# A linear-attention and SoLU kernel: the conversion of the weights, the decay tables, the attention diagonals, the load queues and the order of the last iterations are changed

## The chip, the cores and the metric

The kernel runs on one core of one Trainium2 chip. The core has five engines with a queue of instructions each: TensorE (PE; its weight loads are shown apart as PEld), VectorE (DVE), ScalarE (ACT), GpSimd (POOL) and SyncE (SP), which here only issues transfers. Transfers run on 16 DMA engines. The time is the device time of the program in microseconds (us); the median of three runs before the change is 511.51 us (511.32 to 512.56).

## The reference, cut to what matters

```python
batch, n_heads, seq, head_dim = (4, 8, 768, 48)       # r, k, v
n_tokens, d_model, d_ff = (3072, 384, 1024)           # w_in, w_out, g_ln: float64 weights, float32 gain
...
for t in range(S):
    cur = np.einsum('bhd,bhe->bhde', u[None] * kt, vt)
    y[:, :, t] = np.einsum('bhd,bhde->bhe', rt, state + cur)
    state = w[None, :, :, None] * state + np.einsum('bhd,bhe->bhde', kt, vt)
...
h = x @ w_in
e = np.exp(h - h_max)
solu = h * e / (np.sum(e, axis=-1, keepdims=True) + 1e-09)
ln = (solu - mu) / np.sqrt(var + 1e-06) * g_ln
return (ln @ w_out).astype(np.float32)
```

First a linear attention with a decay w per head and channel runs over 768 steps of four sequences. Its output, 3072 tokens of 384, goes through a feed-forward block: a matmul to 1024, an activation h·softmax(h), a layer norm with a gain, and a matmul back to 384. The two weight matrices arrive as 64-bit floats and are turned into 32-bit ones on the chip.

## The kernel before

The work is cut into 24 units of 128 tokens: unit i is one sequence (b) and one chunk (c) of the 768 steps, with c in the outer loop, so that four units of one chunk follow each other. `direct_path` holds everything that runs; another path is entered at the end only if a decay lies outside 0.75 to 1.25.

Ahead of the loop, tables are built (lines 537 to 556). `wd` holds the decay, one channel to a partition, loaded by two transfers of single words. Squarings give its powers `pw`; `back` is the decay to the powers 127 down to 0, built by doubling its columns seven times; `fore` is the reciprocal of `back` times the decay; `kdec` is `back` transposed on PE.

Each unit passes these steps:

- `load` (454): k, r and v of the unit on SP's queue, 192 KB each in rows of 192 bytes.
- `weigh` (592): POOL forms `kp`, the weighted keys (596), and `rku` (600, 601); DVE sums it to `own` (603); POOL writes `AT`, a diagonal of `own` for each of eight heads (605).
- `turn` (608): PE transposes r (`tr_ps`) and kp (`tk_ps`); DVE scales the first by `fore` into `rT` (615), ACT copies the second into `kT` (619).
- `scores` (622): 16 small matmuls into two tiles `at`; DVE copies what lies above the diagonal into `AT` (632).
- `finish` (635): the matmuls `y_ps` from the state (643) and from `AT` and v (648), an ACT copy to `x` (652), the matmuls `kv_ps` (656) and the new state.
- `turn_x` (665): transposes of x, and an ACT copy to `xT` (671).
- `ffn_in` (673): 12 matmuls of 512 columns into `h_ps` (678); then maximum, exp, sum and product on DVE and ACT, with two one-column steps on POOL, into `solu`.
- `turn_ln` (700): transposes of `solu` (`t_ps`), and copies to `lnT` on DVE (708) and ACT (710).
- `ffn_out` (712): matmuls of 384 columns into `o_ps` (717), an ACT copy (720) and a store on SP's queue (721).

The loop (730) runs i from -2 to 31 and does these steps for different units: the attention of unit i, `ffn_in` five units behind (LA) and `ffn_out` another three behind (LO). So the feed-forward input of unit 0 comes in iteration 5, the output in iteration 8, and the attention ends in iteration 23. PE's order is the order in which the program is written (`manual_schedule`, 729). On the other engines and queues the framework's scheduler chooses the order by the program's order and by what it takes to be ready; each runs its list strictly in that order.

Between `turn` and `ffn_in`, iterations from -1 on convert two pieces of the weights each (738): six pieces of w_in (128 x 512) and then eight of w_out (128 x 384). A raw piece comes by a transfer on ACT's queue (495) into one of five buffers; `convert` (497) takes the exponent and mantissa out of the two 32-bit words with seven DVE instructions, and POOL adds the low part (521, 523) and, for w_out, multiplies by the gain (524).

## Time and profile before

| | |
|---|---|
| median of three runs | 511.51 us |
| the profiled execution | 512.92 us |
| its span, first to last instruction | 511.1 us |
| busy PE / PEld / DVE / ACT / POOL | 440.5 / 304.0 / 263.8 / 119.5 / 189.0 us |
| the same, share of the span | 86 / 59 / 52 / 23 / 37 % |
| mean granted clock of PE | 0.938 of 2.4 GHz |
| moved by DMA | 25.84 MB, 50 GB/s of HBM over the span |

The span is shorter than the profiled execution by 1.8 us, which lie around it. The page cuts the span in 40 slices and writes a digit for each engine and slice, the busy share in tenths (9 is 90% or more). The granted clock is given in the same way: 9 stands for full speed, 5 for half. "Idle before, releaser" names what ended an engine's idle time. A chain of waits leads from the last instruction back to what released each step.

### The profile page before, as it was taken

What the parts mean: (1) busy time and instruction counts of PE and PEld (TensorE: products, weight loads), DVE (VectorE), ACT (ScalarE), POOL (GpSimd) and SP (SyncE); (2) the same over time, 40 slices, a digit from 0 to 9 for tenths busy, and PEclk for the clock granted to TensorE, in tenths of its full rate; (3) what the DMA queues carried; (4) which work ended last, traced back from release to release, by engine and by line L of the source; (5) the groups of instructions that cost most, each with busy time, mean ns of one, the idle gap of its engine ahead of it and who ended that gap; (6) DMA issues with size and microseconds to landing.
All of it is one profiled execution on the core that took longest, in us unless ns stands there. A gap on an engine that the chain in (4) does not pass through costs nothing.

```text
span 511.1 us, 5767 instructions
## 1 busy us (share of the span) xinstructions
PE 440.5 (86%) x2220; PEld 304.0 (59%) x2220; DVE 263.8 (52%) x441; ACT 119.5 (23%) x217; POOL 189.0 (37%) x193
## 2 busy tenths in 40 slices
PE   0147776795999999999999999999999898888995
PEld 0137766772777757766776667666765564444453
DVE  4999999996763443345244425432443123333310
ACT  0110001012242332322232223222322222222211
POOL 2797668589554235324532442232000000000000
PEclk9995557597999999999999999999999999999999
DMA  9972436122222022212211221000000000000001
GB/s 193 249 135 58 112 91 149 33 48 47 48 47 62 16 47 62 49 29 47 63 37 36 51 48 32 1 17 15 17 2 14 15 17 15 16 11 5 15 32 38
DMA packets 81991, 25.84 MB, mean 51 GB/s; under 512 B 76961, under 2 KB 80162, under 8 KB 81954
## 3 DMA queue, kind: packets, MB, share of 16 engines
q1 hardware_dynamic: 78336, 18.88, 17.8%
q10 hardware_dynamic: 3618, 6.50, 4.2%
q8 instruction: 19, 0.31, 0.3%
q14 instruction: 18, 0.15, 0.1%
HBM read 20.65 MB, written 4.72 MB: 50 GB/s over the span
## 4 chain that ended last, share of the span: by engine, by line
PE 68%; DVE 22%; DMA 4%; POOL 2%; ACT 1%; issue 1%; ACTq 0%; DVEq 0%; POOLq 0%
PE o_ps L717 25%; PE h_ps L678 22%; PE y_ps L648 6%; PE at L629 3%; PE y_ps L643 3%; PE kv_ps L656 3%; PE t_ps L706 2%; DVE low L518 2%; DVE st L682 2%; DVE ex L507 2%; DVE ma L515 2%; DVE ma L517 2%; DVE ex L508 2%; DVE ex L510 2%; DVE AT L632 2%; DMA rpad<-in_r_dram 2%
## 5 line engine op out<-in xcount | busy, mean ns | idle before, releaser
L678 PE MATMUL h_ps<-w_in_sb,xT 128*128 128x512 f32 x288 | 129.9, 601 | 10.3 <-DVE solu L688 5.9
L717 PE MATMUL o_ps<-w_out_sb,lnT 128*128 128x384 f32 x384 | 130.3, 492 | 8.0 <-DVE lnT L708 8.0
L717 PEld LDWEIGHTS o_ps<-w_out_sb,lnT 128*128 128x128 f32 x384 | 71.0, 190 | 56.8 <-DVE lnT L708 10.5
L678 PEld LDWEIGHTS h_ps<-w_in_sb,xT 128*128 128x128 f32 x288 | 53.4, 192 | 70.6 <-issue 64.4
L693 POOL TENSOR_SCALAR st<-st 128x1 f32<-128x1 f32 x24 | 4.6, 192 | 206.6 <-ACT sq L692 206.3
L682 DVE TENSOR_REDUCE st<-h_ps 128x1 f32<-128x1024 f32 x24 | 29.4, 1223 | 75.4 <-PE h_ps L678 75.4
L605 POOL TENSOR_TENSOR AT<-ident,own 128x1024 f32<-128x1024 f32 x24 | 46.5, 1938 | 46.2 <-PE y_ps L648 41.7
L648 PE MATMUL y_ps<-vt,AT 128*128 128x48 f32 x384 | 54.3, 302 | 0.0
L648 PEld LDWEIGHTS y_ps<-vt,AT 128*128 128x128 f32 x384 | 52.9, 221 | 0.8 <-issue 0.7
L629 PE MATMUL at<-rT,kT 48*128 48x128 f32 x384 | 35.2, 318 | 18.2 <-DVE AT L632 18.1
L696 DVE TENSOR_SCALAR solu<-solu,st 128x1024 f32<-128x1024 f32 x24 | 20.8, 869 | 54.6 <-POOL st L695 54.6
L629 PEld LDWEIGHTS at<-rT,kT 48*128 48x128 f32 x384 | 29.6, 215 | 25.5 <-DVE AT L632 15.4
L710 ACT COPY lnT<-t_ps 128x512 f32<-128x512 f32 x24 | 14.1, 586 | 121.6 <-PE t_ps L706 121.0
L692 ACT ACTIVATE sq<-solu,st 128x1024 f32<-128x1024 f32 x24 | 27.5, 1148 | 51.7 <-DVE st L690 51.7
L596 POOL TENSOR_TENSOR kp<-kpad,kdec 128x512 f32<-128x512 f32 x24 | 34.2, 1428 | 12.4 <-PE kv_ps L656 12.4
L632 DVE COPY_PREDICATED AT<-later,at 128x512 f32<-128x512 uint32 x48 | 33.5, 724 | 1.8
L603 DVE TENSOR_REDUCE own<-rku 128x8 f32<-128x384 f32 x24 | 13.1, 545 | 38.6 <-POOL rku L601 38.6
L652 ACT COPY x<-y_ps 128x384 f32<-128x384 f32 x24 | 11.5, 479 | 90.4 <-PE y_ps L648 90.4
L688 DVE SCALAR_TENSOR_TENSOR solu<-h_ps,st,e 128x1024 f32<-128x1024 f32 x24 | 30.8, 1284 | 0.8
L684 ACT ACTIVATE e<-h_ps,st 128x1024 f32<-128x1024 f32 x24 | 26.9, 1119 | 15.4 <-DVE st L682 15.4
L706 PEld LDWEIGHTS t_ps<-ident,solu 128*128 128x128 f32 x192 | 22.5, 141 | 12.0 <-issue 10.2
L600 POOL TENSOR_TENSOR rku<-kpad,u_bc 128x384 f32<-128x384 f32 x24 | 25.6, 1066 | 9.6 <-DMA kpad<-in_k_dram 9.1
(67 smaller groups left out, 489.6 us busy)
## 6 DMA issues: line engine op xcount, KB each, us to landing
kpad<-in_k_dram SPq DMA_DIRECT2D x24, 192.0 KB, 3.5
rpad<-in_r_dram SPq DMA_DIRECT2D x24, 192.0 KB, 3.3
vt<-in_v_dram SPq DMA_DIRECT2D x24, 192.0 KB, 2.9
out_dram<-o SPq DMA_DIRECT2D x24, 192.0 KB, 1.9
raw<-in_moe_w_in_dram ACTq DMA_DIRECT2D x6, 512.0 KB, 6.2
raw<-in_moe_w_out_dram ACTq DMA_DIRECT2D x8, 384.0 KB, 3.8
u_bc<-in_u_dram ACTq DMA_DIRECT2D x1, 192.0 KB, 3.9
wd<-in_w_dram ACTq DMA_DIRECT2D x2, 0.8 KB, 6.0
```

Source lines behind the costliest of these rows:

```text
L596: nc.gpsimd.tensor_mul(kp.rearrange("p h d -> p (h d)"), kt.rearrange("p h d -> p (h d)"), kdec.rearrange("p a d -> p (a d)"))
L605: nc.gpsimd.tensor_mul(AT, ident.unsqueeze(1).to_broadcast([128, H, T]), own.to_broadcast([128, H, T]))
L629: nc.tensor.matmul(pss[q][:, a, :], X["kT"][rows, a, :], X["rT"][rows, a, :], start=True, stop=True)
L632: nc.vector.copy_predicated(A4[:, :, q, :], later.to_broadcast([128, HP, T]), pss[q])
L648: nc.tensor.matmul(y_ps[:, h, :], AT[:, h, :], vt[:, h, :], start=first, stop=(h == H - 1), skip_group_check=True)
L678: nc.tensor.matmul(h_ps[:, ts(n, NX)], X["xT"][:, j, :], w_in_sb[:, j, ts(n, NX)], start=(j == 0), stop=(j == KD - 1))
L682: nc.vector.tensor_reduce(out=nmax, in_=h_ps, axis=AX.X, op=ALU.max, negate=True)
L684: nc.scalar.activation(out=e, in_=h_ps, func=ACT.Exp, bias=nmax, accum_out=se)
L688: nc.vector.scalar_tensor_tensor(out=solu, in0=h_ps, scalar=rs, in1=e, op0=ALU.mult, op1=ALU.mult, accum_out=tot)
L692: nc.scalar.activation(out=sq, in_=solu, func=ACT.Square, bias=nmu, accum_out=ss)
L706: nc.tensor.transpose(t_ps[:, f, :], X["solu"][:, ts(4 * g + f, 128)], ident)
L717: nc.tensor.matmul(o_ps, X["lnT"][:, f, :], w_out_sb[:, f, :], start=(f == 0), stop=(f == KF - 1))
```

## The change

- The conversion clamps the absolute value of the high word as a 32-bit float (ACT, DVE), shifts and merges it (two DVE instructions), scales the low word to an integer (ACT) and adds the two as integers (POOL). The gain of w_out is multiplied on ACT.
- One piece is converted per iteration, and three, three and two in iterations 5, 6 and 7. Raw pieces are loaded on SP's queue among k, r and v, three ahead instead of five, one further from iteration -2 on.
- The decay is loaded in contiguous rows (`wq`) at the head of SP's queue and transposed on PE. The powers and their reciprocals fill both tables, `back` and `fore`, in the same doubling steps. `kdec` is copied on ACT, `wt` on DVE.
- The range check of the decay moves into iteration 10.
- ACT writes the diagonals of `AT` in eight instructions, one for each head.
- `turn_ln` comes before `ffn_in` up to iteration 28; from there, one unit earlier, it comes before `ffn_out`.

```diff
@@ -428,6 +428,8 @@
     LA, LO = 5, 3
     LOW, HIGH = 0.75, 1.25
 
+    FLOOR, CEIL = 2.0 ** -15, 122880.0
+
     const = ctx.enter_context(tc.tile_pool(name="const", bufs=1))
     apool = ctx.enter_context(tc.tile_pool(name="apool", bufs=2))
     fpool = ctx.enter_context(tc.tile_pool(name="fpool", bufs=2))
@@ -451,31 +453,21 @@
         nc.vector.memset(kpads[i][:, :, D:P], 0.0)
         nc.vector.memset(rpads[i][:, :, D:P], 0.0)
 
-    def load(i):
+    def load(i, which="krv"):
         b, c = units[i]
-        for t, src in ((kpads, k), (rpads, r), (vts, v)):
-            nc.sync.dma_start(out=t[i % len(t)][:, :, 0:D],
-                              in_=src[b, :, ts(c, T), :].rearrange("h s d -> s h d"))
-
-
...
-    nc.vector.memset(wd, 1.0)
-    for q in range(2):
-        nc.scalar.dma_start(out=wd[q * P : q * P + D, :, 0],
-                            in_=w.rearrange("(a q) d -> q d a", q=2)[q])
-    load(0)
-    nc.scalar.dma_start(out=u_bc.rearrange("p h d -> p (h d)"),
-                        in_=u.rearrange("h d -> (h d)").partition_broadcast(128))
-    load(1)
-    load(2)
-    load(3)
-    nc.scalar.dma_start(out=g_sb, in_=moe_g_ln.rearrange("(c p) -> p c", p=128))
-    nc.scalar.dma_start(out=wrow, in_=w.rearrange("h d -> (h d)").partition_broadcast(1))
+    nc.vector.memset(wq, 1.0)
 
 
     def words(x):
@@ -492,40 +484,51 @@
     def load_weights(j):
         dst, src, _ = pieces[j]
         raws[j] = wpool.tile([128, dst.shape[1], 2], U32, tag="raw", name="raw", bufs=5)
-        nc.scalar.dma_start(out=raws[j].rearrange("p n o -> p (n o)"), in_=src)
+        nc.sync.dma_start(out=raws[j].rearrange("p n o -> p (n o)"), in_=src)
 
     def convert(j):
         dst, _, f = pieces[j]
         n = dst.shape[1]
         raw = raws.pop(j)
         lo, hi = raw[:, :, 0], raw[:, :, 1]
-        bias = (1023 - 127) << 20
-        ex = wpool.tile([128, n], U32, tag="ex", name="ex")
+        mag = wpool.tile([128, n], F32, tag="mag", name="mag")
         ma = wpool.tile([128, n], U32, tag="ma", name="ma")
-        low = wpool.tile([128, n], F32, tag="low", name="low")
-
-        nc.vector.tensor_single_scalar(out=ex, in_=hi, scalar=0x7FF00000, op=ALU.bitwise_and)
-        nc.vector.tensor_scalar(out=ex, in0=ex, scalar1=float(bias),
-                                scalar2=float(bias + (255 << 20)), op0=ALU.max, op1=ALU.min)
-        nc.vector.tensor_scalar(out=ex, in0=ex, scalar1=float(bias), scalar2=8.0,
-                                op0=ALU.subtract, op1=ALU.mult)
-        nc.vector.scalar_tensor_tensor(out=ex, in0=hi, scalar=0x80000000, in1=ex,
+        low = wpool.tile([128, n], U32, tag="low", name="low")
+
+
+        nc.scalar.activation(out=mag, in_=hi.bitcast(F32), func=ACT.Abs)
+        nc.vector.tensor_scalar(out=mag, in0=mag, scalar1=FLOOR, scalar2=CEIL,
+                                op0=ALU.max, op1=ALU.min)
+
+
+        nc.vector.tensor_scalar(out=ma, in0=mag.bitcast(U32), scalar1=3, scalar2=0x3FFFFFF8,
+                                op0=ALU.logical_shift_left, op1=ALU.bitwise_and)
+        nc.vector.scalar_tensor_tensor(out=ma, in0=hi, scalar=0xC0000000, in1=ma,
                                        op0=ALU.bitwise_and, op1=ALU.bitwise_or)
 
-        nc.vector.tensor_scalar(out=ma, in0=hi, scalar1=3, scalar2=0x007FFFF8,
-                                op0=ALU.logical_shift_left, op1=ALU.bitwise_and)
-        nc.vector.tensor_tensor(out=ma, in0=ma, in1=ex, op=ALU.bitwise_or)
-        nc.vector.scalar_tensor_tensor(out=low, in0=lo, scalar=2.0 ** -52, in1=ex.bitcast(F32),
-                                       op0=ALU.mult, op1=ALU.mult)
+        nc.scalar.activation(out=low, in_=lo, func=ACT.Copy, scale=2.0 ** -29)
         if f is None:
-            nc.gpsimd.tensor_add(dst, ma.bitcast(F32), low)
+            nc.gpsimd.tensor_tensor(out=dst.bitcast(U32), in0=ma, in1=low, op=ALU.add)
         else:
-            nc.gpsimd.tensor_add(low, ma.bitcast(F32), low)
-            nc.gpsimd.tensor_scalar(out=dst, in0=low, scalar1=g_sb[:, f : f + 1], scalar2=1.0,
-                                    op0=ALU.mult, op1=ALU.mult)
-
-    for j in range(5):
-        load_weights(j)
+            nc.gpsimd.tensor_tensor(out=ma, in0=ma, in1=low, op=ALU.add)
+            nc.scalar.activation(out=dst, in_=ma.bitcast(F32), func=ACT.Copy,
+                                 scale=g_sb[:, f : f + 1])
+
+
+    nc.sync.dma_start(out=wq[:, :, 0:D], in_=w.rearrange("(a q) d -> a q d", q=2))
+    load(0, "kr")
+    nc.scalar.dma_start(out=u_bc.rearrange("p h d -> p (h d)"),
+                        in_=u.rearrange("h d -> (h d)").partition_broadcast(128))
+    load(1, "kr")
+    load(0, "v")
+    load_weights(0)
+    load(1, "v")
+    load(2)
+    load_weights(1)
+    load(3)
+    load_weights(2)
+    nc.scalar.dma_start(out=g_sb, in_=moe_g_ln.rearrange("(c p) -> p c", p=128))
+    nc.scalar.dma_start(out=wrow, in_=w.rearrange("h d -> (h d)").partition_broadcast(1))
 
...
@@ -534,26 +537,29 @@
 
 
 
-    back = const.tile([128, HP, T], F32, name="back")
-    fore = const.tile([128, HP, T], F32, name="fore")
-    pw = const.tile([128, 8, HP, 1], F32, name="pw")
+    tab = const.tile([128, 2, HP, T], F32, name="tab")
+    back, fore = tab[:, 0], tab[:, 1]
+    pw = const.tile([128, 2, 8, HP], F32, name="pw")
+    wd_ps = psM.tile([128, HP], F32, tag="m", name="wd_ps")
+    nc.tensor.transpose(wd_ps, wq.rearrange("a q d -> a (q d)"), ident[0:HP, 0:HP])
     nc.vector.memset(back[:, :, T - 1 : T], 1.0)
-    nc.vector.tensor_scalar(out=pw[:, 0], in0=wd, scalar1=LOW, scalar2=HIGH,
+    nc.vector.tensor_scalar(out=pw[:, 0, 0], in0=wd_ps, scalar1=LOW, scalar2=HIGH,
                             op0=ALU.max, op1=ALU.min)
     for j in range(7):
+        nc.vector.tensor_mul(pw[:, 0, j + 1], pw[:, 0, j], pw[:, 0, j])
+    nc.vector.reciprocal(out=pw[:, 1], in_=pw[:, 0])
+    nc.vector.tensor_copy(out=fore[:, :, T - 1 : T], in_=pw[:, 1, 0].unsqueeze(2))
+    for j in range(7):
         n = 1 << j
-        step = pw[:, j].to_broadcast([128, HP, n])
-        nc.vector.tensor_mul(back[:, :, T - 2 * n : T - n], back[:, :, T - n : T], step)
-        nc.vector.tensor_mul(pw[:, j + 1], pw[:, j], pw[:, j])
-    nc.vector.tensor_mul(fore, back, pw[:, 0].to_broadcast([128, HP, T]))
-    nc.vector.reciprocal(out=fore, in_=fore)
+        step = pw[:, :, j].unsqueeze(3).to_broadcast([128, 2, HP, n])
+        nc.vector.tensor_mul(tab[:, :, :, T - 2 * n : T - n], tab[:, :, :, T - n : T], step)
 
 
     kdec = const.tile([128, HP, 128], F32, name="kdec")
     kd_ps = psM.tile([128, HP, 128], F32, tag="m", name="kd_ps")
     for a in range(HP):
         nc.tensor.transpose(kd_ps[:, a, :], back[:, a, :], ident)
-    nc.vector.tensor_copy(out=kdec, in_=kd_ps)
+    nc.scalar.copy(out=kdec, in_=kd_ps)
 
 
...
@@ -564,24 +570,27 @@
     nc.vector.tensor_copy(out=later[:, 0, :], in_=mf)
 
 
...
     wt = const.tile([128, HP, 2, D], F32, name="wt")
     nc.gpsimd.memset(wt, 0.0)
     for q in range(2):
         rows = slice(q * P, q * P + D)
-        nc.gpsimd.tensor_copy(out=wt[rows, :, q, :], in_=pw[rows, 7].to_broadcast([D, HP, D]))
+        nc.vector.tensor_copy(out=wt[rows, :, q, :],
+                              in_=pw[rows, 0, 7].unsqueeze(2).to_broadcast([D, HP, D]))
     states = [const.tile([128, HP, 2, D], F32, name=f"state{b}") for b in range(B)]
+
+    bad = flag.tile([1, 1], mybir.dt.int32, name="bad")
+
+    def check_range():
+
...
     live = {}
 
@@ -602,8 +611,8 @@
         own = small.tile([128, H, 1], F32, name="own")
         nc.vector.tensor_reduce(out=own[:, :, 0], in_=rku, axis=AX.X, op=ALU.add)
         AT = X["AT"] = apool.tile([128, H, T], F32, name="AT", bufs=4)
-        nc.gpsimd.tensor_mul(AT, ident.unsqueeze(1).to_broadcast([128, H, T]),
-                             own.to_broadcast([128, H, T]))
+        for h in range(H):
+            nc.scalar.activation(out=AT[:, h, :], in_=ident, func=ACT.Copy, scale=own[:, h])
 
     def turn(i):
         X, rt = live[i], rpads[i % NLD]
@@ -723,7 +732,8 @@
 
     N = len(units)
     todo = list(range(len(pieces)))
-    ahead = 5
+    count = {5: 3, 6: 3, 7: 2}
+    ahead = 3
     weigh(0)
     weigh(1)
     with tc.manual_schedule(engines={mybir.EngineType.PE}):
@@ -735,18 +745,22 @@
                 weigh(i + 3)
             if 0 <= i + 2 < N:
                 turn(i + 2)
-            for _ in range(2):
+            for _ in range(count.get(i, 1)):
                 if i >= -1 and todo:
                     convert(todo.pop(0))
-                    if ahead < len(pieces):
-                        load_weights(ahead)
-                        ahead += 1
+                if ahead < len(pieces):
+                    load_weights(ahead)
+                    ahead += 1
+            if i == 10:
+                check_range()
+            if 0 <= l < N and i < N + LA:
+                turn_ln(l)
             if 0 <= j < N:
                 ffn_in(j)
-            if 0 <= l < N:
-                turn_ln(l)
             if 0 <= i + 1 < N:
                 scores(i + 1)
+            if N + LA - 1 <= i < N + LA + LO - 1:
+                turn_ln(l + 1)
             if 0 <= l < N:
                 ffn_out(l)
             if 0 <= i < N:
```

## Rows read from the trace of the kernel before

**Rows 1.** The page, 40 slices: busy tenths of DVE, granted clock of PE.
```profile
DVE  4999999996763443345244425432443123333310
PEclk9995557597999999999999999999999999999999
```

**Rows 2.** Stretches: us, busy PE, PEld, DVE, ACT, POOL, then clock, DMA, GB/s.
```profile
30.66:103.75 73.09, 54.91 (x288) 51.24 (x288) 72.99 (x103) 6.98 (x13) 53.03 (x40) 0.63 0.41 94
103.75:121.01 17.26, 11.35 (x74) 7.87 (x72) 17.25 (x27) 3.23 (x6) 15.22 (x15) 0.89 0.33 61
133.97:145.26 11.29, 11.29 (x71) 8.02 (x72) 7.10 (x13) 3.92 (x8) 6.92 (x8) 1.00 0.27 53
145.26:385.41 240.15, 238.92 (x1309) 163.71 (x1307) 100.66 (x177) 70.28 (x128) 81.35 (x88) 1.00 0.16 37
385.41:505.65 120.24, 109.20 (x406) 63.00 (x406) 34.03 (x61) 29.86 (x55) 5.19 (x14) 1.00 0.04 16
```

**Rows 3.** The chain that ended last, its start: from, length, what.
```profile
6.06 5.43 DMA wd<-in_w_dram
...
29.20 1.42 POOL kp L596
30.66 1.11 PE tk_ps L618 x4
```

**Rows 4.** Timeline of PE, 38 to 104 us: start, length, group.
```profile
53.01 2.69 PE L629 MATMUL at<-rT,kT 48*128 48x128 f32 x16 [2.58 <-DVE AT L632]
...
67.13 2.68 PE L629 MATMUL at<-rT,kT 48*128 48x128 f32 x16 [4.41 <-DVE AT L632]
...
77.78 1.77 PE L629 MATMUL at<-rT,kT 48*128 48x128 f32 x16 [1.18 <-DVE AT L632]
79.47 3.56 PE L648 MATMUL y_ps<-vt,AT 128*128 128x48 f32 x16
```

**Rows 5.** Waits, in total: us, times, longest.
```profile
DVE own L603 <- POOL rku L601: 38.6, 11, 4.8
...
PE o_ps L717 <- DVE lnT L708: 8.0, 11, 1.0
...
PE h_ps L678 <- ACT xT L671: 4.3, 7, 0.6
```

**Rows 6.** Timeline: the one-row load of w and its reader.
```profile
1.73 0.69 ACTq L478 DMA_DIRECT2D wrow<-in_w_dram  x1
...
5.69 0.35 DVE L569 TENSOR_SCALAR ok<-wrow 1x384 f32<-1x384 f32 x1 [3.61 <-DMA wrow<-in_w_dram]
```

**Rows 7.** Tile pw and its readers: count, ns min/median/max, first and last start.
```profile
L546 DVE TENSOR_TENSOR back<-back,pw x7: 155/276/960, 12.4 to 19.4; 128x4 f32<-128x4 f32 x1, 128x8 f32<-128x8 f32 x1, 128x16 f32<-128x16 f32 x1, 128x32 f32<-128x32 f32 x1
L547 DVE TENSOR_TENSOR pw<-pw x7: 149/150/1869, 13.3 to 19.8; 128x4 f32<-128x4 f32 x7
```

**Rows 8.** Groups by form on ACT, 200 to 340 us.
```profile
L619 ACT COPY kT<-tk_ps 128x512 f32<-128x512 f32 x8 | 4.7, 586 | 3.1 <-PE tk_ps L618 3.1
...
L671 ACT COPY xT<-xt_ps 128x384 f32<-128x384 f32 x8 | 3.8, 480 | 6.3 <-PE xt_ps L669 6.3
```

**Rows 9.** Conversion, groups by form (busy, mean ns): L508 until 40 us, others later.
```profile
L508 DVE TENSOR_SCALAR ex<-ex 128x512 uint32<-128x512 uint32 x2 | 0.8, 409 | 0.0
...
L515 DVE TENSOR_SCALAR ma<-raw 128x512 uint32<-128x512 uint32 x4 | 5.2, 1306 | 0.0
...
L512 DVE SCALAR_TENSOR_TENSOR ex<-raw,ex 128x512 uint32<-128x512 uint32 x4 | 2.7, 678 | 0.0
...
L521 POOL TENSOR_TENSOR w_in_sb<-ma,low 128x512 f32<-128x512 f32 x5 | 7.3, 1470 | 2.8 <-DVE ma L517 2.2 <-DVE low L518 0.6
```

**Rows 10.** POOL's diagonal, line 605: count, ns min/median/max.
```profile
L605 POOL TENSOR_TENSOR AT<-ident,own x24: 1897/1899/2341, 17.1 to 351.0; 128x1024 f32<-128x1024 f32 x24
```

**Rows 11.** The page's DMA queues: packets, MB, share of 16 engines.
```profile
q1 hardware_dynamic: 78336, 18.88, 17.8%
q10 hardware_dynamic: 3618, 6.50, 4.2%
```

More of the change, by code (lines that the diff above doesn't have):

```diff
@@ L452, in direct_path @@
         nc.vector.memset(rpads[i][:, :, D:P], 0.0)
-    def load(i):
+    def load(i, which="krv"):
         b, c = units[i]
-        for t, src in ((kpads, k), (rpads, r), (vts, v)):
-            nc.sync.dma_start(out=t[i % len(t)][:, :, 0:D],
-                              in_=src[b, :, ts(c, T), :].rearrange("h s d -> s h d"))
-    wd = const.tile([128, HP, 1], F32, name="wd")
+        for t, src, n in ((kpads, k, "k"), (rpads, r, "r"), (vts, v, "v")):
+            if n in which:
+                nc.sync.dma_start(out=t[i % len(t)][:, :, 0:D],
+                                  in_=src[b, :, ts(c, T), :].rearrange("h s d -> s h d"))
+    wq = const.tile([HP, 2, P], F32, name="wq")
     u_bc = const.tile([128, H, D], F32, name="u_bc")
```

19 lines of the change are left out of this document (9 added, 10 removed).

## The prediction

> **What bounds the kernel now.** Read first the two slice lines [rows 1]: VectorE (DVE) stands at 9 from slice 1 to slice 8, about 102 us, and the granted TensorE clock is at 5 in slices 3 to 5 and 7. After that the clock is at 9 and DVE at 3 to 5. So the run has a front bound by DVE and a body bound by TensorE (PE). The stretches say it sharper [rows 2]: from the first transpose of a weighted key (30.66) to the first matmul of the feed-forward part (103.75) DVE is busy 72.99 of 73.09 us and PE 54.91, at a mean clock of 0.63. From 145.26 to 385.41 PE is busy 238.92 of 240.15 us: nothing else can shorten that stretch. From 385.41 to the last matmul's end PE idles 11.04 of 120.24 us. Ahead of all this lies the start: the chain waits for the decay row w until 6.06 + 5.43 = 11.49, and PE's steady work begins at 30.66 [rows 3].
>
> In the front PE waits at the scores for the masked copy on DVE (4.41 us before the matmuls at 67.13 [rows 4]), and DVE is full because each weight piece costs it seven instructions. In the drain the waits are named [rows 5]: o_ps for the DVE copy of lnT, 8.0 us in 11 waits, and h_ps for the ACT copy of xT, 4.3 us in 7.
>
> Beyond 0.3% (1.5 us) a measurement of this kernel can tell a change from none.
>
> **Part 1, the start.** The old w load scatters single words and lands at 11.49, queued on ACT's queue behind raw weights; the new one has contiguous rows and is first on SP's queue. The nearest row is the contiguous load of the same w into one row: issued at 1.73, its reader released at 5.69, so 4.0 us [rows 6]. Issued near 0.8, wq is there near 5. Then: a transpose with its hand-over, some 0.4; clamp, seven squarings, reciprocal and copy, ten at 0.15 (the least time of a squaring [rows 7]); seven table steps over both tables. The old steps have a median of 0.28 and 0.16 at least [rows 7]; at twice the width I take 2.1 for the seven. That is 9. Four transposes of back (1.1), the ACT copy (0.59 [rows 8]) and kp on POOL (1.42 [rows 3]) with hand-overs give the first tk_ps near 12.5 instead of 30.66: 18 us earlier. Bounds: 11, if w lands in 3 us; 18, if k, r and the first raw pieces share the DMA engines as they do now and hold kp back. The long reciprocal, whose result the first scaled query needs, falls away with this. The range check of w moves to iteration 10, inside the PE-bound stretch, where DVE is busy 100.66 of 240.15 us [rows 2]: nothing. With it goes no transfer; the copies into wt pass from POOL to DVE, where DVE now has nothing to convert yet: nothing.
>
> **Part 2, the conversion.** Seven DVE instructions become three: clamp 0.41, shift-and-mask 0.41, merge 0.68, together 1.5 us where the old seven are some 3.7 (four at 0.41, three at 0.68 [rows 9]). ACT gains two of about 0.59 [rows 8]; POOL keeps one addition at 1.47, now on integers, and loses the scaling of w_out to ACT. The integer add has no row. The float add on the same tiles is the nearest, 1.47, and I take that; a gain is not excluded but worth nothing while POOL is not the bound, and twice it, 3 us, is the other end, with which POOL would still stay below 9.7 a unit in the front.
>
> Only one piece per iteration is now converted in the front. What bounds an iteration there? The stretch 133.97 to 145.26 holds an iteration with no conversion but with a feed-forward input [rows 2], so it bounds from above: DVE 7.10 + 1.5 = 8.6; POOL 6.92 less the diagonal's 1.9 [rows 10] plus 1.5 = 6.5; ACT 3.92 plus diagonals and two conversions (2.1 + 1.2) = 7.2, of which exp and square are not there yet. DMA: 17.8% of 511 us over 24 units is 3.8, one piece is 4.2% over 14, or 1.5 [rows 11]: 5.3 a unit. PE takes 9.7 at 1.2 GHz (from 53.01 without a gap until the wait of 4.41 ahead of 67.13 begins, at 62.7 [rows 4]) and about half at 2.4. So PE becomes the bound, and its clock decides. The rows: a gapless 9.7 us from 53.01 stayed at 1.2 GHz; after a like run from 67.13 the scores at 77.78 took 1.77 against 2.68 us, partly at 2.4, and the y_ps behind them ran at 1.2 again [rows 4]. I take alternation: 10 us at 1.2 GHz, then some 4 at 2.4, in which POOL's pace lets PE do 9.7 / 6.5 = 1.5 times as much, so (10 + 6) / 14 = 1.14. PE's work from tk_ps to the first h_ps is 54.9 us as played [rows 2]; over 1.14 that is 48.1, and 1.4 more for the part that already ran at 2.4: 49.5. First h_ps: 12.5 + 49.5 = 62, against 103.75: **-41.75**. Bounds: 51.5 (full clock, POOL's 6.5 over six iterations) and 70 (1.2 GHz throughout).
>
> **Part 3, iterations 5 to 7** (three, three and two w_out pieces; no output matmuls yet). Now 103.75 to 145.26, 41.5 us. PE's floor is 11.29 each [rows 2]. DVE without delays: 7.1 + 4.5 = 11.6 twice, then PE's 11.3: 34.5. But in 103.75 to 121.01 DVE was full for 17.25 us with two pieces: (17.25 - 7.10) over 14 instructions is 0.72 each [rows 2]. With nine, nine and six such: 13.6, 13.6, 11.4, sum 38.6. The delay comes from POOL: a shift of 512 columns averages 1.31 where the like clamp took 0.41 [rows 9], and a 4-column squaring went from 0.15 to 1.87 [rows 7], the length of POOL's diagonal, 1.90 [rows 10]. The Trainium skill, SBUF — State Buffer, section "Who interferes with whom", has VectorE and GpSimd share one port pair as an exclusive lock, held for a whole instruction. By that rule the remaining kp, rku and integer adds go on blocking DVE, and the sum would be the 38.6, two us more than I take; without it 34.5. POOL is lighter by the diagonal, so I take 36.5: **-5**.
>
> **Part 4, diagonals on ACT.** Eight copies of 128 columns. From 480 ns at 384 and 586 at 512 columns [rows 8] a copy is 0.85 ns a column plus 0.155: 0.26 each, 2.1 a unit; bounds 1.9 (overlap) and 3 (the scale read from SBUF). ACT has room: 70.28 of 240.15 us are busy [rows 2]. Its order matters: the copies of x, xT and kT queue behind them. What covers a late xT is now turn and turn_ln, about 1.7 us of PE. I take 0, up to 0.7 a unit over 16 units for the range.
>
> **Part 5, queues.** Raw loads leave ACT's queue and stand on SP's ahead of later k, r, v. Each waits for its buffer, hence for a conversion, and those loads with it. Four units are loaded ahead and a turn comes two iterations after its load, so I take 0; one late conversion costs its 1.5. With ACT's queue rid of 14 raw loads, its copies wait for no issue.
>
> **Part 6, the drain.** turn_ln moves ahead of ffn_in: its transposes fill the wait for xT, and lnT has the whole ffn_in to be copied. Its two copies pass ffn_in's maximum and exp on DVE and ACT, which start only when h_ps is complete, 5 us later. From iteration 28 it comes one unit earlier. Both waits go, 12.3 us [rows 5] (11.04 of it idle inside the drain's stretch [rows 2], the rest at its edge); some 0.7 more since PE need not refill after each. **-13**; bounds 9 (the copies now meet buffers still being emptied) and 14. Next late is nothing: exp and sums run under the output matmuls. The last copy and store stay.
>
> **Sum.** The profiled execution took 512.92 us (span 511.1), 1.4 above the median 511.51. 512.92 - 41.75 - 5 - 13 = 453.2; against the median, **452 us**.
>
> **Rivals.**
> A, clock full through the front: PE would be dense from 12 us on, which speaks for it; the fall after 77.78 [rows 4], behind a wait of 1.18, speaks against. First h_ps near 51.5: **441**. Chance 0.20.
> B, clock at 1.2 GHz until the first h_ps, as the run from 53.01 did: h_ps at 70, **460**. Chance 0.18.
> C, ACT's diagonals delay the copies a little, 1 us a unit over 16: **468**. For: one in-order queue; against: ACT is 29% busy there. Chance 0.10.
> D, it does not do what it says: the integer add costs POOL 3 us or the raw loads hold up k and r, so the front keeps another bound, h_ps at 85: **475**. Chance 0.04.
> E, slower. The eight diagonals stand at the head of ACT's queue waiting for own, behind rku and the r load; xT waits behind them and PE behind xT. DVE's own waits for rku up to 4.8 us [rows 5]. With 2.1 of work behind it and 1.7 of cover that is 5.2 a unit and over 16 units 83: **535**. It decides from 60/16 = 3.75 us a unit. Against it: those waits, 38.6 us in 11, average 3.5, and they end because the engine has nothing else to do. Chance 0.04.
>
> **How the numbers follow.** Forecast 0.44. The low end is A with a drain of 14 and an undelayed part 3: 438. The high end takes in B and C and D's size: 476. Outside lie E and the tails of A and D, some 0.15. Faster: all but E and a sliver, 0.95; within 0.3%: 0.01; slower 0.04.
>
> **What would show it.** First tk_ps near 12.5; first h_ps at 62; DVE no longer at 9 in slices 2 to 7, PE there instead with a clock between 0.5 and 0.9; the third h_ps after it 36 us on; 17.2 us a unit in the body; no wait of o_ps on lnT nor of h_ps on xT in the drain, 12 us an iteration there. Wrong if h_ps first starts above 75, if ACT's copies appear as releasers of PE in the body, or if POOL's add exceeds 3 us.

## The result, and the profile after

The changed kernel takes 457.61 us (456.19 to 458.64, four runs) beside 512.03 us: ratio 0.8936, 95% interval 0.8902 to 0.8969. The forecast was 452, with a range of 438 to 476. The profiled execution took 458.56 us, span 456.7. Two of E6's four runs, two of E9's seven (the profiled one among them) and one each of E10's and E11's six were slowed by the state of the chip, and the medians given below for these four are those of the other runs. The changed kernel was run again for E11, and the trace of that execution (454.57 us) is shown beside the first, because the two differ where the forecast was weakest.

The stages are cut where the prediction cut them: at the first `tk_ps`, the first `h_ps`, the fourth `h_ps`, the eighteenth, and the end of PE's last matmul.

| stage, us | before | forecast | after | after, second execution |
|---|---|---|---|---|
| start, until the first tk_ps | 30.66 | 12.5 | 20.90 | 19.56 |
| front, until the first h_ps | 73.09 | 49.5 | 43.00 | 36.65 |
| iterations 5 to 7 | 41.51 | 36.5 | 42.75 | 44.76 |
| body, fourteen units | 240.15 | 240.15 | 238.38 | 240.07 |
| drain | 120.23 | 107.2 | 106.23 | 106.22 |

Two slice lines of the page after, the answer to [rows 1]:

```profile
DVE  5648887987443443443443443533443233333410
PEclk9999799999999999999999999999999999999998
```

DVE stands at 7 to 9 only until slice 9 now. The stretches of after (columns as in [rows 2]):

```profile
20.90:36.60 15.70, 15.70 (x84) 14.31 (x84) 7.25 (x13) 9.15 (x25) 8.39 (x8) 1.00 0.80 190
...
50.00:57.20 7.20, 7.20 (x43) 6.98 (x44) 5.80 (x9) 4.10 (x11) 5.37 (x6) 0.56 1.10 224
...
20.90:63.90 43.00, 40.63 (x288) 37.66 (x289) 31.00 (x49) 27.49 (x71) 27.23 (x24) 0.92 0.86 174
63.90:106.65 42.75, 37.16 (x223) 25.27 (x222) 37.42 (x61) 30.66 (x77) 32.08 (x33) 0.96 0.54 97
106.65:345.03 238.38, 238.38 (x1308) 162.91 (x1307) 103.23 (x178) 96.47 (x227) 57.56 (x74) 1.00 0.16 35
345.03:451.26 106.23, 105.28 (x400) 61.94 (x398) 33.97 (x61) 29.48 (x55) 5.19 (x14) 1.00 0.05 18
```

In the front DVE went from 72.99 of 73.09 us to 31.00 of 43.00, and PE is busy 40.63: the bound changed hands as forecast. The body is PE alone. In the drain 0.95 us of idle PE is left. But in 63.90 to 106.65 PE is busy only 37.16 of 42.75 us, and DVE 37.42, where the prediction had in each iteration an engine that is always full.

### The profile page after: what moved, and what is told of

Same layout as the page of the kernel before. It is cut to its first block, busy times and chain, and to the rows that moved or that the text cites. A ratio compares the mean times of both kernels' runs of the same rounds, so it can differ in the third digit from the quotient of the medians.

```text
span 456.7 us, 5931 instructions
## 1 busy us (share of the span) xinstructions
PE 423.7 (93%) x2221; PEld 289.5 (63%) x2221; DVE 219.5 (48%) x386; ACT 191.2 (42%) x446; POOL 130.9 (29%) x159
## 4 chain that ended last, share of the span: by engine, by line
PE 76%; DVE 11%; ACT 5%; issue 3%; POOL 3%; DMA 1%; ACTq 0%; POOLq 0%
PE h_ps L687 24%; PE o_ps L726 23%; PE y_ps L657 8%; PE at L638 5%; PE t_ps L715 4%; PE kv_ps L665 3%; PE y_ps L652 3%; PE tk_ps L627 2%; PE tr_ps L623 2%; ACT AT L615 1%; DVE solu L697 1%; ACT e L693 1%; PE xt_ps L678 1%; DVE st L691 1%; DVE ma L504 1%
## 5 line engine op out<-in xcount | busy, mean ns | idle before, releaser
L615 ACT ACTIVATE AT<-ident,own 128x128 f32<-128x128 f32 x192 | 60.6, 391 | 10.1 <-DVE own L612 10.0
L657 PE MATMUL y_ps<-vt,AT 128*128 128x48 f32 x384 | 49.5, 285 | 0.0
L657 PEld LDWEIGHTS y_ps<-vt,AT 128*128 128x128 f32 x384 | 48.0, 203 | 0.7 <-issue 0.4
L605 POOL TENSOR_TENSOR kp<-kpad,kdec 128x512 f32<-128x512 f32 x24 | 30.8, 1287 | 43.3 <-PE kv_ps L665 40.4
L638 PEld LDWEIGHTS at<-rT,kT 48*128 48x128 f32 x384 | 25.7, 200 | 18.0 <-issue 13.9
L638 PE MATMUL at<-rT,kT 48*128 48x128 f32 x384 | 31.0, 300 | 2.4 <-DVE AT L641 2.4
L610 POOL TENSOR_TENSOR rku<-rku,rpad 128x384 f32<-128x384 f32 x24 | 24.5, 1021 | 23.4 <-DMA rpad<-in_r_dram 22.8
L715 PE MATMUL t_ps<-ident,solu 128*128 128x128 f32 x192 | 25.2, 273 | 2.0 <-DVE st L699 1.9
```

The lines of the kernel that those rows point to most:

```text
L605: nc.gpsimd.tensor_mul(kp.rearrange("p h d -> p (h d)"), kt.rearrange("p h d -> p (h d)"), kdec.rearrange("p a d -> p (a d)"))
L615: nc.scalar.activation(out=AT[:, h, :], in_=ident, func=ACT.Copy, scale=own[:, h])
L638: nc.tensor.matmul(pss[q][:, a, :], X["kT"][rows, a, :], X["rT"][rows, a, :], start=True, stop=True)
L657: nc.tensor.matmul(y_ps[:, h, :], AT[:, h, :], vt[:, h, :], start=first, stop=(h == H - 1), skip_group_check=True)
L715: nc.tensor.transpose(t_ps[:, f, :], X["solu"][:, ts(4 * g + f, 128)], ident)
```

## The experiments

Each ran beside the kernel before on its chip (E1 to E4 513.05 us, E5 to E8 513.10, E9 to E12 512.47). "Changed" is the changed kernel, 0.8936.

**E1, the drain alone**, on the kernel before:

```diff
+            if 0 <= l < N and i < N + LA:
+                turn_ln(l)
             if 0 <= j < N:
                 ffn_in(j)
-            if 0 <= l < N:
-                turn_ln(l)
             if 0 <= i + 1 < N:
                 scores(i + 1)
+            if N + LA - 1 <= i < N + LA + LO - 1:
+                turn_ln(l + 1)
```

> The kernel before with nothing but the new order of turn_ln (ahead of ffn_in up to iteration 28, one unit early from there). If the two named waits of the drain are all that this part buys and it is independent of the rest, the stretch from the h_ps of unit 17 to PE's end shrinks from 120.2 to about 106 us and the time falls by 14 to 498. Rival: part of the 14 us comes from ACT and POOL being relieved by the other edits; then this alone gives 6 to 8 us, about 505.

Measured: 498.71 us, 0.9719 (0.9698 to 0.9739). The drain is 106.21, the body 238.38, and the eighteenth `h_ps` comes where it came before, at 385.5. The reorder is a gain by itself, some 14 us. It also lengthens iterations 5 to 7, from 41.51 to 43.37 us: the eight `t_ps` transposes of unit 0 (1.04 us, at 146.26) now stand ahead of the fourth `h_ps` and not behind it, and the second `h_ps` group takes 8.10 us where it took 6.86. Of the waits on `lnT` and `xT` [rows 5] 0.9 us is left; this is the view of PE's waits from 345 us on in the changed kernel, whose drain is the same, and there the `h_ps` come 12.0 us apart (386.53, 398.54):

```profile
PE h_ps L687 <- ACT xT L680: 0.9, 4, 0.2
```

**E2, the conversion alone**, on the kernel before, two pieces in each iteration as there:

```diff
-        nc.vector.tensor_single_scalar(out=ex, in_=hi, scalar=0x7FF00000, op=ALU.bitwise_and)
...
-            nc.gpsimd.tensor_add(dst, ma.bitcast(F32), low)
+        nc.scalar.activation(out=mag, in_=hi.bitcast(F32), func=ACT.Abs)
...
+            nc.gpsimd.tensor_tensor(out=dst.bitcast(U32), in0=ma, in1=low, op=ALU.add)
```

> The kernel before with only the new conversion (two pieces per iteration, raw loads still on ACT's queue, diagonals still on POOL). If DVE's seven instructions per piece bounded the front, DVE now needs 3.2 + 2 x 1.5 = 6.2 us a unit without delays, PE with its clock takes over, the stretch from the first tk_ps to the first h_ps falls from 73.1 to about 50 us and the time to about 488. Rival: the port that DVE and POOL share keeps DVE full, since POOL still writes the diagonals (1.9 us each) and every DVE instruction beside it is held up; then the stretch stays above 60 us and the time above 498.

Measured: 491.84 us, 0.9587 (0.9564 to 0.9610). First `tk_ps` at 20.68, front 60.83, iterations 5 to 7 41.04. So the front shrank by 12.3 and stayed above 60, as the rival had it; the time still fell below the rival's 498, because the start shrank too, by 10.0, which neither had. The old tables, the scattered load of w (its reader starts at 11.41) and the long reciprocal are all still there. What is gone from the start are the conversion steps among DVE's table steps, and two diagonals and an addition of a piece ahead of the first `kp` in POOL's list: `kdec` is copied at 18.65 where it was at 26.35, and `kp` follows within 0.8 us where it took 2.8. The share of each was not measured.

**E3, diagonals back on POOL**, in the changed kernel:

```diff
-        for h in range(H):
-            nc.scalar.activation(out=AT[:, h, :], in_=ident, func=ACT.Copy, scale=own[:, h])
+        nc.gpsimd.tensor_mul(AT, ident..., own...)
```

> The changed kernel with the diagonals back on POOL. Theory: in iterations 5 to 7 the eight diagonals and the scaling of w_out stand ahead of exp in ACT's queue and hold up solu and the next h_ps; without them the stretch from the first to the fourth h_ps falls from 42.75 to about 38 us, while the front (43.0 us) grows by some 3 us because POOL holds DVE up again: time 455 to 458. Rival: ACT's queue is not the cause and the diagonals on POOL only add delays on DVE; then both stretches grow, 42.75 to 46 and 43 to 48, time 465. In both the body stays at 17.2 us a unit.

Measured: 472.01 us, 0.9197 (0.9163 to 0.9231). Start 25.93, front 45.30, iterations 5 to 7 48.19, body 238.38. The move to ACT is worth some 13 us (0.9197 / 0.8936 = 1.029), in all three early stages (5.0, 2.3 and 5.4), and the body neither gains nor pays. So the rival came, and the time went beyond it, because the start grew as well. In iterations 5 to 7 PE's longest wait, with the diagonals on POOL:

```profile
PE h_ps L687 <- DVE solu L697: 6.1, 2, 3.4
```

**E4, two pieces in every iteration**, the pacing of before in the changed kernel:

```diff
-    count = {5: 3, 6: 3, 7: 2}
-            for _ in range(count.get(i, 1)):
+            for _ in range(2):
```

> The changed kernel with two conversions in every iteration, so that all but the last are done before the first h_ps. If the eight w_out conversions between the first and the fourth h_ps cost the 9 us by which that stretch (42.75) exceeds PE's 33.9, it falls to 35 to 37 us, the front grows by at most 4 us, and the time is about 454. Rival: the stretch is held up by the diagonals in ACT's queue and by own waiting for POOL, with or without conversions; then it stays at 40 us or more, the front still grows, and the time is 460 or more.

Measured: 460.25 us, 0.8980 (0.8960 to 0.9000). Front 46.78, iterations 5 to 7 41.61: their sum is 88.39 against 85.75, or 81.41 in the second execution, which shares the start of E4 (first `tk_ps` at 19.52). The time and the stage are the rival's, but its reason is not: the last pieces (three) are converted between the first `h_ps` and the second, and in the two stretches behind that PE is busy all the time, though `rku`, `own` and the diagonals (72, 80 and 88 ahead of the first three exp) are there as ever:

```profile
82.84:95.83 12.99, 12.99 (x71) 8.63 (x72) 7.83 (x15) 5.47 (x14) 7.83 (x9) 0.87 0.01 2
95.83:107.91 12.08, 12.08 (x82) 8.81 (x81) 7.47 (x14) 6.94 (x18) 5.81 (x8) 1.00 0.33 63
```

What they take beyond PE's 11.29 [rows 2] is PE's own work: in the first an `h_ps` group of 7.12 us instead of 5.32, beside a clock of 0.50 until 86.33, in the second 1.04 us of `t_ps`.

**E5, the powers in PSUM, squared by ACT:**

```diff
-    pw = const.tile([128, 2, 8, HP], F32, name="pw")
+    pw = psM.tile([128, 2, 8, HP], F32, tag="m", name="pw")
-        nc.vector.tensor_mul(pw[:, 0, j + 1], pw[:, 0, j], pw[:, 0, j])
+        nc.scalar.activation(out=pw[:, 0, j + 1], in_=pw[:, 0, j], func=ACT.Square)
```

> The changed kernel, with the powers of w held in PSUM and squared on ACT, so that DVE's table steps read one operand from PSUM and DVE makes no squaring in SBUF. Theory: the start is late (first tk_ps 20.9 where 12.5 was forecast) because DVE's small squarings and table steps stand in SBUF beside POOL's rku, 494 and 550 ns each instead of some 150 to 300; out of POOL's way the first tk_ps comes near 17, and the whole run at 453.5 us against 457.6. Rival: their length is their own and not POOL's doing, or the chain of POOL's kp and the transposes sets the start anyway: first tk_ps stays at 20 or later and the time within 1.5 us of 457.6.

Measured: 461.36 us, 0.8984 (0.8948 to 0.9019); first `tk_ps` 22.13. The rival came, and the run is some 4 us longer than the changed kernel. Timeline of DVE in this kernel, around the table steps:

```profile
13.76 0.37 DVE L550 RECIPROCAL pw<-pw 128x32 f32<-128x32 f32 x1 [1.34 <-ACT pw L549]
...
14.36 1.63 DVE L555 TENSOR_TENSOR tab<-tab,pw 128x8 f32<-128x8 f32 x6
16.84 0.55 DVE L612 TENSOR_REDUCE own<-rku 128x8 f32<-128x384 f32 x1 [0.85 <-POOL rku L610]
17.31 0.68 DVE L555 TENSOR_TENSOR tab<-tab,pw 128x512 f32<-128x512 f32 x1
```

Six steps take 1.63 us, but DVE waited 1.34 for ACT's squares before, and the sum `own` stands ahead of the seventh step in DVE's list and waits for POOL: what the steps save is spent waiting.

**E6, weighing after the feed-forward input**, meant to put the diagonals behind exp on ACT:

```diff
-            if 0 <= i + 3 and i + 3 < N and i + 3 >= 2:
+            if 0 <= i + 3 and i + 3 < N and i + 3 >= 2 and i < 5:
                 weigh(i + 3)
...
+            if 5 <= i and i + 3 < N:
+                weigh(i + 3)
```

> The changed kernel, but from iteration 5 on a unit's keys and queries are weighed, with their eight diagonals on ACT, only after that iteration's feed-forward input has been issued. Theory: the iterations 5 to 7 take 42.75 us because the eight diagonals wait for own behind POOL's rku at the head of ACT's queue and hold up the scaling of w_out and, through it, DVE's e; behind exp they hold up nothing, the three iterations take 37 to 38 us and the whole run 453 us. Rival: the loop of st, e, solu and the one h_ps buffer, stretched by DVE's conversions and by POOL, sets the pace: the three stay above 41 us, and the run within 1.5 us of 457.6 or slower, since the weighing now comes later in each unit.

Measured: 457.96 us (455.39 and 460.52), with two more runs at 462.40 and 464.74. 457.96 / 513.10 is 0.8925; the recorded ratio is 0.9011 (0.8963 to 0.9060). Either way there is no gain over the changed kernel. Iterations 5 to 7 take 45.39 in the profiled execution, which starts like E11 (first `tk_ps` at 19.73) and is to be read beside its 44.76. The numbers are the rival's, but the edit did not do what it was meant to: the scheduler kept the diagonals ahead of exp on ACT. Ahead of the first three exp of the feed-forward part stand 71, 80 and 88 diagonals, in the changed kernel 72, 80 and 88. ACT ahead of the first of them:

```profile
65.77 1.86 ACT L615 ACTIVATE AT<-ident,own 128x128 f32<-128x128 f32 x6 [1.11 <-DVE own L612]
...
68.98 1.09 ACT L693 ACTIVATE e<-h_ps,st 128x1024 f32<-128x1024 f32 x1
```

So whether the place of the diagonals on ACT matters in these iterations was not tried.

**E7, the old conversion** in the changed kernel, so with one piece an iteration in the front and 3, 3, 2 after it:

```diff
-        nc.scalar.activation(out=mag, in_=hi.bitcast(F32), func=ACT.Abs)
...
+        nc.vector.tensor_single_scalar(out=ex, in_=hi, scalar=0x7FF00000, op=ALU.bitwise_and)
...
```

> The changed kernel with the seven-instruction conversion of the kernel before in place of the new one. Theory: the conversion is what filled DVE in the front, and beside the other parts it is worth what it was worth alone (21 us): the stretch from the first tk_ps to the first h_ps goes from 43.0 back to 62 or more, body and drain stay at 238.4 and 106.2, and the run takes some 479 us. Rival: with the diagonals off POOL the old conversion is no longer held up, its seven instructions run at 0.4 to 0.7 us each, and the front grows by 8 us or less: some 466 us.

Measured: 474.54 us, 0.9240 (0.9206 to 0.9275), between both. Start 23.96, front 44.37, but iterations 5 to 7 54.07, with PE waiting there for DVE:

```profile
PE h_ps L689 <- DVE solu L699: 10.3, 2, 7.5
```

At one piece an iteration even seven instructions fit into the front: it grows by the rival's "8 us or less", by 1.4. The price of the old form moved with its pieces into iterations 5 to 7. There DVE is busy 49.21 us instead of 37.42, but POOL too, 40.34 instead of 32.08, so this run does not part the two.

**E8, the range check held back**, and **E10, the same again** beside the changed kernel:

```diff
-    wrow = const.tile([1, dm], F32, name="wrow")
...
     def check_range():
+        wrow = wpool.tile([1, dm], F32, tag="raw", name="wrow", bufs=5)
+        nc.sync.dma_start(out=wrow, in_=w.rearrange("h d -> (h d)").partition_broadcast(1))
```

> The changed kernel, with the row for the range check of w loaded only where the check stands, at iteration 10, into a buffer of the raw weights, so that the check cannot be moved to the start. Theory: the check's six instructions at the start (5.73 to 8.36) stood ahead of the clamp of w; without them the first tk_ps comes 1.3 us earlier, at 19.6, and the time falls by as much, to 456.3 us. Rival: the chain from tables over kp to tk_ps is set by POOL's rku and by loads, and nothing changes within 0.5 us; a transfer of 1 row at iteration 10 costs nothing in either case.

> The late check again, beside the changed kernel on the same chip. Theory: the check moved to iteration 10 makes the run 1.5 to 3 us shorter than the changed kernel, the first tk_ps stands near 19.5. Rival: the 455.06 beside 457.61 was the chip and the runs; both are within 1 us of each other here.

Measured: 455.06 us, 0.8872 (0.8839 to 0.8906), then 456.99 us, 0.8932 (0.8890 to 0.8974), beside 457.17 for E11. The first looked like the theory; the repetition did not hold it up. The first `tk_ps` stood at 19.49 and 19.52, but so it did, at 19.56, in E11 with the check at the start.

**E9, one iteration more for w_out**, on top of E8:

```diff
-    LA, LO = 5, 3
+    LA, LO = 5, 4
-    count = {5: 3, 6: 3, 7: 2}
+    count = {5: 2, 6: 2, 7: 2, 8: 2}
```

> The kernel of the late check (wrow loaded only at iteration 10), and the output part of a unit one iteration later (LO 4 instead of 3, with as many solu buffers), so that w_out is needed one iteration later and its eight pieces are converted two in each of the iterations 5 to 8 instead of 3, 3 and 2 in 5 to 7. Theory: what remains in iterations 5 to 7 is the loop st, e, solu over the one h_ps buffer, stretched by each conversion that stands among its steps on DVE, ACT and POOL; with two pieces it takes 12.5 us, as the second and third iteration of the run with two conversions each did (13.0, 12.1), so from the first h_ps to the fourth after it 50 us instead of 45.5 + 17.2 less the 5.9 of the output matmuls that move behind it; the run takes 4 to 5 us less than the late check alone, about 450.5. Rival: the loop takes as long with two pieces as with three (diagonals, rku and kp hold it up): four iterations of 14 to 15, the work left undone then costs as much as it saves, and the time is that of the late check alone within 1.5 us, or more.

Measured: 458.33 us, 0.8954 (0.8926 to 0.8982). The rival's time: no gain over E8 and E10. In the profiled execution the `h_ps` follow one another by 13.8, 14.3, 15.9 and 12.1 us. But the engines lag behind the program's order, and what is converted in these four is 3, 2, 3 and no pieces, not two each. PE waits 5.3 us for `solu` in the first three and for nothing in the fourth.

**E11, the changed kernel again, unedited.**

> The changed kernel itself, unedited. If the front's length (43.0 from the first tk_ps to the first h_ps) is a property of the program, it comes out again within 1 us, with TensorE at its lower level until 36 us. If it hangs on when the clock rises, which small shifts decide, another front comes, between 36.7 and 43, with iterations 5 to 7 longer when the front is shorter; the time within 456 to 460 us either way.

Measured: 457.17 us (454.47 to 457.30), 0.8907 (0.8878 to 0.8936). Start and front are not the same as in the first trace: the second case came, a little past its figures (front 36.65). More below.

**E12, raw weights loaded on ACT's queue** again:

```diff
-        nc.sync.dma_start(out=raws[j]..., in_=src)
+        nc.scalar.dma_start(out=raws[j]..., in_=src)
```

> The changed kernel with the loads of the raw weights back on ACT's queue. Theory (they were costed at nothing): the time stays within 1.5 us of the changed kernel, and the stages within 2 us. Rival: on SP's queue they let ACT go on without issuing 14 loads, each waiting for its buffer, at the place where ACT is busiest; back on ACT's queue the front or the iterations 5 to 7 grow, and the run takes 461 us or more.

Measured: 466.25 us, 0.9081 (0.9048 to 0.9114), 9 us more than E11 on the same chip. The rival's time, though most of it at another place than it said: first `tk_ps` 28.91 (E11: 19.56), front 38.60 (36.65), iterations 5 to 7 47.41 (44.76). POOL's first steps on the second unit, in E12 and then in the changed kernel:

```profile
12.91 0.99 POOL L609 TENSOR_TENSOR rku<-kpad,u_bc 128x384 f32<-128x384 f32 x1 [6.04 <-DMA kpad<-in_k_dram]
```

```profile
8.77 0.99 POOL L609 TENSOR_TENSOR rku<-kpad,u_bc 128x384 f32<-128x384 f32 x1 [1.57 <-DMA kpad<-in_k_dram]
```

Three raw pieces issued on ACT's queue from 1.25 on are under way together with k, r and w: k of the second unit takes 8.90 us (3.95 to 12.85, in the chain of waits), and the transpose of w starts at 10.72 instead of 7.12. That is 3.6 of the 8 us by which the first `tk_ps` is later than in the first execution. The rest comes after w has landed: among DVE's table steps now stand the three conversion steps of the first piece (17.71, 19.00 and 22.02) and those of the range check, and the tables are done at 25.71, 15 us after w and not 10.6. Nor is it ACT's queue as such: in E2 the raw pieces are on it too, but one ahead of w and four from 6.92 on, and the first `tk_ps` comes at 20.68.

No version here beats the changed kernel by more than the runs differ.

## Why the prediction was right, and where it was not

The total was met within 1.3%, with terms that partly cancel: that the total came so close is in part luck. Against the forecast of 453.2 for the profiled execution: start +8.4, front -6.5, iterations 5 to 7 +6.25, body -1.8, drain -1.0, together +5.4, which is 458.56.

**Part 1, the start: too early by 8.4 us, outside its bounds of 11 to 18.** That w would land earlier was right (PE's wait for it ends at 7.12, DVE's ended at 11.49), but by itself it did not bring the first `tk_ps` forward: E2 has the old load and the same 20.68. Three terms failed in size. The landing of w, "near 5", is 7.12, because its transfer is not at the head of SP's queue: it waits for DVE's memset of `wq` (1.99) and is issued third, behind k and r.

```profile
2.18 1.53 SPq L518 DMA_DIRECT2D wq<-in_w_dram  x1
```

"Ten at 0.15", from the clamp to the copy, took the row of an undisturbed squaring; in the first execution these steps, with two sums `own` among them, run from 8.42 to 13.86. DVE and POOL in the two executions of the same changed kernel, the first and then E11:

```profile
8.60 3.48 DVE L549 TENSOR_TENSOR pw<-pw 128x4 f32<-128x4 f32 x6
...
9.72 1.94 POOL L610 TENSOR_TENSOR rku<-rku,rpad 128x384 f32<-128x384 f32 x2
...
13.86 3.85 DVE L555 TENSOR_TENSOR tab<-tab,pw 128x8 f32<-128x8 f32 x7
```

```profile
7.83 1.14 DVE L549 TENSOR_TENSOR pw<-pw 128x4 f32<-128x4 f32 x6
...
9.04 0.99 POOL L609 TENSOR_TENSOR rku<-kpad,u_bc 128x384 f32<-128x384 f32 x1 [1.50 <-DMA kpad<-in_k_dram]
...
11.02 0.55 DVE L612 TENSOR_REDUCE own<-rku 128x8 f32<-128x384 f32 x1 [2.04 <-POOL rku L610]
```

Six squarings take 3.48 us where POOL forms `rku` from 8.77 to 11.66 beside them, and 1.14 where POOL starts only at 9.04. This agrees with the Trainium skill, SBUF — State Buffer, "Who interferes with whom", where the two engines share one port pair under an exclusive lock, and a DVE instruction with two SBUF inputs contends with a GpSimd instruction that reads SBUF. The prediction used that for iterations 5 to 7 and forgot it for the start. But the second execution spends most of what it saved in the wait of 2.04 for `own`, and E5 shows the same. The seven table steps, 2.1 in the sum, took 3.85 and 3.06. What the sum did not contain at all is POOL's list and DVE's waits for it. And "the range check moves to iteration 10" did not come true: the scheduler placed it at the start, from 5.73 on. In the first execution it is done only at 8.36, and the clamp of w, ready at 7.35, waits behind it; in E11 the clamp starts at 7.64. E8 and E10, without the check there, start as E11 does (19.49 and 19.52 beside 19.56), so it is not what sets the start.

**Part 2, conversion and front: right in kind, too long by 6.5 to 12.9 us.** PE became the bound and its clock decides; the alternation between its two levels is there. A conversion takes DVE 2.49 us for 512 columns (0.96, 0.85 and 0.68) instead of 1.5. POOL's integer add is 1.28 where 1.47 was taken, no penalty. What failed is the rate of 1.14: PE does in 40.63 us, and in E11 in 34.41, what took it 54.91 [rows 2], which is 1.35 and 1.60 times as fast, since it spends more of the front at its upper level. `y_ps` of sixteen matmuls and `tk_ps` of four in the timeline of PE, first the first execution, then E11:

```profile
29.58 3.65 PE L657 MATMUL y_ps<-vt,AT 128*128 128x48 f32 x16
...
37.98 1.99 PE L657 MATMUL y_ps<-vt,AT 128*128 128x48 f32 x16
...
51.10 3.65 PE L657 MATMUL y_ps<-vt,AT 128*128 128x48 f32 x16
```

```profile
21.32 1.06 PE L627 MATMUL tk_ps<-ident,kp 128*128 128x128 f32 x4
24.07 0.60 PE L627 MATMUL tk_ps<-ident,kp 128*128 128x128 f32 x4
...
38.54 2.55 PE L657 MATMUL y_ps<-vt,AT 128*128 128x48 f32 x16
```

The front of E11, and in it the stretch at 0.50 (columns as in [rows 2]):

```profile
19.56:56.21 36.65, 34.41 (x288) 31.85 (x289) 29.80 (x47) 27.34 (x70) 27.18 (x23) 0.91 1.07 211
39.77:46.60 6.83, 6.83 (x40) 6.28 (x39) 6.83 (x10) 3.94 (x12) 5.09 (x5) 0.50 1.05 197
```

By these lengths the first execution runs at 1.2 GHz from 20.90 until after 29.58 (a `tk_ps` of four still takes 1.06 at 35.66) and again from 51.10 to about 57; E11 reaches 2.4 before 24.07 and falls back once, from 39.77 to 46.60, behind a wait of 2.17 ahead of 37.45. Of the difference of 6.35 us between the fronts 6.22 are busy time of PE. What lets one rise within 4.5 us of its first `tk_ps` and the other only after 14.8 was not settled; the programs are the same. Nor does the term belong to the conversion alone, as the prediction had it: with the old conversion at the new pacing (E7) the front is 44.37. And the 39 us (51.5 - 12.5) that POOL's pace was to set as the least is no floor: E11 is below it.

**Part 3, iterations 5 to 7: the step that failed clearly.** -5 was taken with 34.5 and 38.6 as ends; measured are +1.2 and +3.3. The 38.6, which the prediction had from the delayed DVE instructions, was nearer, but short too. The sum took the fullest engine of each iteration as full, and PE's floor as 11.29. Of the 42.75 us, 3 x 11.29 = 33.9 are that floor [rows 2], and 37.16 - 33.9 = 3.3 are work of PE that the sum had at nothing. Two lines hold nearly all of it:

```profile
78.27 7.02 PE L687 MATMUL h_ps<-w_in_sb,xT 128*128 128x512 f32 x12 [1.20 <-DVE solu L697]
...
106.16 0.66 PE L715 MATMUL t_ps<-ident,solu 128*128 128x128 f32 x4 [1.93 <-DVE st L699]
```

The second `h_ps` group takes 7.02 us where the first takes 5.32: the granted clock is 0.50 from 78.15 to 81.57. And the eight `t_ps` of unit 0, some 1.2 us, stand in this stage because the new order of Part 6 puts them ahead of the fourth `h_ps`; E1 shows it alone. The last 5.6 us are waits, by name:

```profile
PE t_ps L715 <- DVE st L699: 1.9, 1, 1.9
PE h_ps L687 <- DVE solu L697: 1.9, 2, 1.2
PE tk_ps L627 <- ACT x L661: 1.6, 1, 1.6
```

DVE, which the sum had as the bound of iterations 5 and 6, is busy 37.42 us, close to the 38.6, but it idles 5.3, 3.5 of them until POOL's `rku` is there for `own`. E4 shows what the waits hang on: from its second `h_ps` to its fourth no piece is left, PE waits for nothing, and what it takes beyond 11.29 is the clock and `t_ps` again. The fourth stretch of E9, without a piece, shows the same. So the waits come with the pieces; here 3, 3 and 2 are converted between these `h_ps`. By which engine the pieces cause them is open: the old conversion (E7: 54.07) loads DVE and POOL more, and the diagonals on POOL (E3: 48.19) lengthen the stage too, by POOL or by DVE beside it. There is one `h_ps` buffer, and PE's next group waits for maximum, exp and product over DVE, ACT, DVE; the chain of waits leads through that loop:

```profile
69.88 0.97 POOL rku L610
...
70.87 0.56 DVE own L612
71.43 0.02 issue
71.46 2.45 ACT AT L615 x8
73.91 0.51 ACT w_out_sb L514
74.42 1.09 ACT e L693 x2
```

Eight diagonals stand behind `rku` ahead of exp in ACT's queue, which is rival E's mechanism in these iterations. By E4 it makes no wait where there are no pieces. Whether it lengthens the loop where there are was not shown, since E6 left the diagonals where they were. What a version with a second `h_ps` buffer would take was not tried.

**Part 4, diagonals on ACT: right.** Eight take 2.45 us (2.1 forecast, 1.9 to 3 as bounds), 390 ns each:

```profile
L615 ACT ACTIVATE AT<-ident,own 128x128 f32<-128x128 f32 x89 | 27.9, 390 | 1.2 <-DVE own L612 1.1
```

Each is 0.39 where 0.26 was worked out, and eight take less than 8 x 0.39 because they overlap. The copies of [rows 8] read no scale from memory and take their input from PSUM; the diagonals read a scale, which is what the upper end of 3 stood for, and their input from SBUF. No run parts the two. The Trainium skill, ScalarE: Activation LUTs, section "What ACT_TABLE_LOAD costs", has a constant part, one column a cycle and some 93 ns for a scale that is read; an estimate by it for 128 columns is 386 ns, and the trace agrees. In the body PE waits for nothing: PE is busy 238.38 of 238.38 us, so rival C is out. E3's 13 us say that the move earns more than Part 4 gave it, which was 0.

**Part 5, queues: costed at 0, measured 9 us (E12).** The prediction looked at what late conversions hold up on SP's queue, and not at the start, where the move keeps raw pieces behind k, r and w. It had raw pieces that hold kp back as the upper bound of Part 1, and did not see that Part 5 bears on it. With w itself they cost 3.6 us, and the rest of E12's loss came with the order that the scheduler then chose.

**Part 6, the drain: right.** -14.0 against -13, and E1 shows it alone. About 1 us of the 14 is not won but moved: one unit's `t_ps` less in the drain is one more in iterations 5 to 7. The 1.8 us by which the body is shorter, in E1 too, the prediction did not have; PE's idle 1.23 us there [rows 2] are gone. In E11 the body is 240.07 again, but only its first step is longer than in the first execution (18.92 and not 17.22), beside a clock of 0.50 from 101.21 to 104.62.

Rivals A, B and D are out as causes: the clock was neither full nor low throughout the front, the integer add takes 1.28 us and not 3, and the front has PE as its bound. Rival E's 3.75 us a unit did not come: the body is not longer.

## What to carry to other kernels

Before you promise a gain in a stage where more than one engine is nearly full, add three things to the fullest engine's floor: the stretch that PE may spend at its lower level, the work that another part of the change moves into the stage, and the waits; here these were 1.7, 1.2 and 5.6 us of 42.75. Cost a queue move at the start of the kernel too, where the first transfers are under way together; the scheduler's order can change with the move as well. Look into the trace whether the scheduler did what an edit asked: it moved the range check to the start, and it left the diagonals of E6 in their place. And run the kernel twice before believing a difference of 2 or 3 us in a stretch whose clock moves.

## What the runs showed of the hardware that was not expected

- The granted clock column reads 1.00 from 20.90 to 36.60, while sixteen `y_ps` matmuls take 3.65 us there, as at 51.10 where the column stands at 0.56, and 1.99 at 37.98. At the head of a run the durations tell the level, the column does not.
- One program starts in two ways: `rku` of the first unit began at 6.01 or 6.38 us, the first `tk_ps` came at 20.90 or 19.56 and the first `h_ps` at 63.90 or 56.21 (E4, E8 and E10, at 6.20 to 6.25, have a first `tk_ps` at 19.49 to 19.52); iterations 5 to 7 give 2.0 and the body 1.7 of the difference back. That the one follows from the other is not shown.
- An integer add on POOL takes about as long as the float add of the same shape: 1.43 us for 512 columns in E2, where the kernel before has 1.44 over its six pieces. In the changed kernel it is 1.28, and the float add put back there (E7) 1.37, so the surroundings matter as much.
